# Loads that fill both halves of the partitions from the same 64 rows, issued as two transfers instead of one

## The chip, the cores and the metric

The kernel runs on one core of a Trainium2 chip. The metric is the time of one execution in microseconds (us) on the device, as the median of several runs; lower is better. The engines are TensorE (PE, with its weight loads PEld), VectorE (DVE), ScalarE (ACT), GpSimd (POOL) and SyncE (SP). SP does no arithmetic here: it issues every transfer (DMA) of the program, one after the other, and its issues appear in the profile as SPq. 16 DMA engines move the data.

## What is computed

Three parts follow one another: a recurrence with a state of 40 x 40 for each of 32 (batch, head) pairs over 768 steps, and two gated layers over 3072 tokens of 320 values.

```python
# r, k, v, w, a, b: (4, 8, 768, 40), float32
for t in range(S):
    y[:, :, t] = np.einsum('bhd,bhde->bhe', rt, state)
    Sa = np.einsum('bhde,bhe->bhd', state, at)
    state_decay = state * wt[:, :, None, :] - np.einsum('bhd,bhe->bhde', Sa, bt)
    state = state_decay + np.einsum('bhd,bhe->bhde', vt, kt)
# y as (3072, 320) goes into layer 1, its result into layer 2
h = x @ w_in                      # (320, 2048)
g = h * np.clip(h + 3, 0, 6) / 6  # layer 1;  layer 2: g = h / (1 + exp(-h))
out = g @ w_out                   # (2048, 320)
```

The four weight matrices arrive as 64-bit numbers.

## The kernel before

The recurrence is worked in chunks of 32 steps, which turns it into matmuls and one triangular inverse for each chunk and head. Four chunks are a window of 128 steps of two batches (16 heads); there are 12 windows (`NN`) and 48 chunks. For each window:

- `prepare` (lines 299 to 375) loads the inputs of the window (`in_pre`), forms running products of the decay, and writes them to scratch in DRAM (`scr_w`, `scr_a`, `scr_kb`).
- `windows` (434) forms the 64 triangular factors (16 heads x 4 chunks) of 32 x 32 on PE and writes them to `scr_l` as 64 rows of 1024 numbers.
- `factors` (479) loads `scr_l` into `u`, the same 64 rows into partitions 0 to 63 and again into 64 to 127. There are two buffers for `u`; the second lies in the tile `stage`, and its loads read `stage<-scr_l` in the trace. ScalarE (in window 0 also VectorE) copies the even columns for the lower and the odd ones for the upper half into `uh` (line 509 and 506), and VectorE solves the triangles in 60 short instructions (515 and 519). So both halves of the partitions work on one problem, each on every other column.
- `solved` (529) writes the inverses to `scr_t` and loads them into `ga` (line 540). `ga` has three buffers, one for each of three windows in a row.
- `steps` (569) is the recurrence itself. Each chunk begins with matmuls on `rhs` and `ga` (line 602) and ends with the new state in `rhs`; the next chunk needs it. Its small loads are `rhs<-in_vt` (546), `vr<-in_vr` (550) and `ysr<-in_rt` (565).

Beside the recurrence run the conversion of layer 1's weights (`raws` and `convert`, lines 719 to 797: 16 blocks, each with `raw0` from `w_in` and `raw1` from `w_out`, turned from 64-bit numbers into a sum of two float32 ones), `inputs1` (855), which loads a window's result from `scr_y` and its decay from `scr_w` as layer 1's input, and layer 1 itself (`first`, line 927, and `second`, line 971) for the windows that are done. A row of `w_in` or of the input has 320 values, which are two and a half times 128; the last 64 rows are put on both halves of the partitions, so that one matmul over 128 rows can take two products of them. After the last chunk, `phase2` converts layer 2's weights in the same way (`stage<-in_w2i`, `stage<-in_w2o`), while PE finishes layer 1; then layer 2 runs. `raw0` has one buffer in that stage: the load of a block waits until the conversion of the block before has read it.

The order of all instructions is set at build time. Every piece of work is a generator that yields the engine, a cost and the events that it waits for; `Order.run` picks what can start first, then by priority, and emits it. For SP the yielded number is a count of bytes. The planner charges each issue 525 ns of SP and adds the bytes divided by a rate. On the chip each engine, SP included, then takes its instructions strictly in this order, and an instruction that has to wait holds up all behind it.

Four places read a source twice with `unsqueeze(0).to_broadcast([2, ...])`, one transfer for both halves of the partitions: line 489 (12 loads), line 735 (32 loads: 16 blocks in each of the two layers), line 869 (24) and line 874 (12). They are the places of the diff.

Of the kernel before, what the change touches and what calls it, by code (L numbers as in the profile page):

```python
# [20 lines left out]
G = NB * H  # L21
HP = H // 2
NW, WT, CT = 6, 128, 32
NC = WT // CT
# [7 lines left out]
DM, DFF = H * D, 2048  # L32
NM = DFF // 128
MT = NB * WT
# [215 lines left out]
class Kernel:  # L250
# [228 lines left out]
    def factors(self):  # L479

        nc, o = self.nc, self.o
        for n in range(NN):
            k = n % 2 if n > 1 else 0
            u = self.u[k]
            free = [("uo", n - 1) if n < 3 else ("iv", n - 2)] if n else []
            if k:
                free += self.converted
            el = yield ("sp", 524e3, ("lo", n), *free)
            nc.sync.dma_start(out=u.rearrange("p j i -> p (j i)"),
                              in_=self.scr_l[n % 2].unsqueeze(0).to_broadcast([2, G * NC, CT * CT]))  # L490
            o.ev[("u", n)] = o.t["sp"]
            o.ev[("ul", n)] = el

# [225 lines left out]
    def raws(self, wi, wo, key):  # L719

        nc, cv = self.nc, self.cv
        for m in range(NM):
            if wi.dtype == mybir.dt.float32:
                k, wiv, wov = 1, wi, wo
            else:
                k, wiv, wov = 2, wi.bitcast(I32), wo.bitcast(I32)
            cs = slice(m * 128 * k, (m + 1) * 128 * k)
            raw, free = self.slot("raw0", key, m)
            raw = raw.bitcast(wiv.dtype)
            yield ("sp", 131e3 * k, free and ("cv", key, free[0], 0), ("u", 0) if key == 1 and m >= GR else None,  # L730
                   ("uo", NN - 1) if key == 2 else None)
            nc.sync.dma_start(out=raw[:, 0:256 * k].rearrange("p (j f) -> p j f", j=2),
                              in_=wiv[0:256, cs].rearrange("(j p) f -> p j f", p=128))
            e = yield ("sp", 66e3 * k)
            nc.sync.dma_start(
                out=raw[:, 256 * k:384 * k],
                in_=wiv[256:320, cs].unsqueeze(0).to_broadcast([2, 64, 128 * k]))
            self.o.ev[("raw", key, m, 0)] = e
            raw, free = self.slot("raw1", key, m)
            raw = raw.bitcast(wiv.dtype)  # L740
            e = yield ("sp", 164e3 * k, free and ("cv", key, free[0], 1))
            nc.sync.dma_start(out=raw[:, 0:DM * k], in_=wov[m * 128:(m + 1) * 128])
            self.o.ev[("raw", key, m, 1)] = e
# [111 lines left out]
    def inputs1(self):  # L855

        nc, o = self.nc, self.o
        xs = self.xw[0].rearrange("p (j b t) -> p j b t", j=3, b=NB)
        ws = self.xw[1].rearrange("p (j b t) -> p j b t", j=3, b=NB)
        xf, wf = (x.rearrange("p (j n) -> p j n", j=3) for x in self.xw)  # L860
        for n in range(NN):
            free = ("xp", n - 1) if n else ("cv", 1, K0 - 1, 1)
            sw, sy = self.scr_w[n], self.scr_y[n]
            for b in range(NB):
                r = sw[b * DM:(b + 1) * DM, 0:WT]
                yield ("sp", 131e3, ("wo", n), free, ("cv", 1, K0 - 1, 0))
                nc.sync.dma_start(out=ws[:, 0:2, b], in_=r[0:256].rearrange("(j p) t -> p j t", p=128))
                yield ("sp", 66e3)
                nc.sync.dma_start(out=ws[:, 2, b], in_=r[256:DM].unsqueeze(0).to_broadcast([2, 64, WT]))
            g = n * NC + NC - 1  # L870
            e1 = yield ("sp", 262e3, *[("yo", g - q, b) for b in range(NB) for q in (0, 2)])
            nc.sync.dma_start(out=xf[:, 0:2], in_=sy[0:256].rearrange("(j p) b t -> p j (b t)", p=128))
            e = yield ("sp", 131e3)
            nc.sync.dma_start(out=xf[:, 2],
                              in_=sy[256:DM].rearrange("p b t -> p (b t)").unsqueeze(0).to_broadcast([2, 64, MT]))
            xh, xl = self.xh[n % 2], self.xl[n % 2]
            e = yield ("pool", 1750.0, e, e1)
            nc.gpsimd.tensor_tensor(out=xf, in0=xf, in1=wf, op=ALU.mult)
            e = yield ("act", 740.0, e, ("g1", n - 2) if n > 1 else None)
            nc.scalar.activation(out=xh, in_=xf, func=AF.Copy)  # L880
            yield ("pool", 1230.0, e)
            nc.gpsimd.tensor_tensor(out=xl, in0=xf[:, 0:2], in1=xh[:, 0:2].bitcast(F32), op=ALU.subtract)
            e = yield ("pool", 640.0)
            nc.gpsimd.tensor_tensor(out=xh[64:128, 2], in0=xf[64:128, 2], in1=xh[64:128, 2].bitcast(F32),
                                    op=ALU.subtract)
            o.ev[("xp", n)] = o.ev[("x", n)] = e
# [317 lines left out]
```

## Time and profile before

| | us |
|---|---|
| median of 3 runs | 1398.6 |
| lowest and highest of them | 1393.26, 1407.38 |
| the profiled execution | 1414.4 |
| its span, first to last instruction | 1412.6 |
| PE busy in it | 1126.7 (80%) |
| DVE, ACT, POOL busy | 823.1, 636.1, 399.4 |
| mean granted clock of PE | 0.902 |

The profile is of one execution, and all its times are in us from the start of the span. A row of the timeline has the start, the duration, the engine, the line of the kernel, the operation, the tile written and the tiles read; in brackets stands how long the engine was idle before it and what ended the idleness. A row of SPq shows how long the issue took on SP, not how long the transfer took. A row of the windows has for each stretch the busy time of PE, PEld, DVE, ACT and POOL, in this order, with the number of their instructions, the granted clock of PE (1.00 is full speed), the share of the 16 DMA engines' time that was busy, and what they moved.

### The profile page before, as it was taken

The page shows a single profiled execution, that of the slowest core. Times are in us where ns is not written, and L with a number is a line of the kernel's source. Part 1 is how long each engine was busy: PE and PEld are TensorE (multiplying, and loading weights), DVE is VectorE, ACT ScalarE, POOL GpSimd, SP SyncE. Part 2 cuts the span into 40 slices and gives each one's busy share as a digit, 9 for nine tenths or more (in the row PEclk, how much of TensorE's full clock was granted, in tenths as well). Part 3 has the DMA queues.
Part 4 walks back from the last instruction along what each step waited for, and adds up shares of the span by engine and source line. Part 5 has one row for each costly group of instructions (what it writes and reads, how often), then busy time and mean ns, then how long its engine had stood idle before and what let it go on. Part 6 is the DMA issues. An engine that isn't in the chain of part 4 may idle for free. (4 is left out here: it accounts for less than half of the span.)

```text
span 1412.6 us, 31488 instructions
## 1 busy us (share of the span) xinstructions
PE 1126.7 (80%) x12278; PEld 1048.3 (74%) x12278; DVE 823.1 (58%) x1948; ACT 636.1 (45%) x1369; POOL 399.4 (28%) x485
## 2 busy tenths in 40 slices
PE   2035348877878877989768989997789999999998
PEld 1034247777778766877767878887779999999997
DVE  6495857557578784965877968458882222322221
ACT  3224435643533534655244456655663333433333
POOL 6333443515324231333331413346550000000000
PEclk9999667879988967997888899999999999999999
DMA  6566765534676564375765743345441000100000
GB/s 198 153 149 151 176 144 118 111 103 112 153 175 142 126 163 124 82 151 151 175 140 129 169 106 97 87 102 111 108 94 44 21 21 22 40 24 21 22 10 22
DMA packets 276414, 150.03 MB, mean 106 GB/s; under 512 B 176032, under 2 KB 257568, under 8 KB 276256
## 3 DMA queue, kind: packets, MB, share of 16 engines
q1 hardware_dynamic: 276256, 147.92, 43.7%
q8 instruction: 99, 1.62, 0.5%
q14 instruction: 59, 0.48, 0.1%
HBM read 113.24 MB, written 34.63 MB: 105 GB/s over the span
## 5 line engine op out<-in xcount | busy, mean ns | idle before, releaser
L971 PE MATMUL po<-w,gh 128*128 128x320 f32 x1536 | 400.5, 328 | 22.7 <-ACT xo L987 19.7
L927 PE MATMUL ph<-xh,w 128*128 128x256 f32 x2304 | 387.5, 298 | 26.9 <-DVE t L942 26.0
L927 PEld LDWEIGHTS ph<-xh,w 128*128 128x128 f32 x2304 | 330.2, 201 | 37.8 <-DVE t L942 28.8
L971 PEld LDWEIGHTS po<-w,gh 128*128 128x128 f32 x1536 | 281.3, 199 | 32.0 <-ACT xo L987 21.5
L971 PE MATMUL po<-w,gl 128*128 128x320 f32 x768 | 248.2, 323 | 11.1 <-DVE gl L953 7.1
L953 DVE TENSOR_TENSOR gl<-t,gh 128x512 fp32r<-128x512 f32 x118 | 88.9, 756 | 246.7 <-ACT gh L947 246.4
L947 ACT ACTIVATE gh<-t 128x512 fp32r<-128x512 f32 x192 | 120.8, 630 | 99.4 <-DVE t L942 90.0
L927 PE MATMUL ph<-xl,w 128*128 128x256 f32 x768 | 164.5, 297 | 0.0
L971 PEld LDWEIGHTS po<-w,gl 128*128 128x128 f32 x768 | 153.3, 200 | 14.9 <-DVE gl L953 10.3
L950 POOL TENSOR_TENSOR gl<-t,gh 128x512 fp32r<-128x512 f32 x74 | 95.2, 1288 | 183.5 <-ACT gh L947 149.8
L944 ACT ACTIVATE t<-ph 128x512 f32<-128x512 f32 x96 | 57.2, 596 | 186.8 <-PE ph L927 186.8
L519 DVE TENSOR_TENSOR uh<-uh,ut 128x30 f32<-128x30 f32 (+4 forms) x360 | 129.2, 359 | 10.5
L643 DVE STREAM_TRANSPOSE vr<-r 64x128 f32<-64x128 f32 x192 | 61.2, 319 | 125.0 <-ACT ysl L619 47.7
L927 PEld LDWEIGHTS ph<-xl,w 128*128 128x128 f32 x768 | 127.3, 201 | 2.5 <-issue 0.3
L602 PE MATMUL r<-rhs,ga 104*32 104x40 f32 x1536 | 75.1, 215 | 63.0 <-DMA ga<-scr_t 30.5
L602 PEld LDWEIGHTS r<-rhs,ga 104*32 104x32 f32 x1536 | 68.1, 123 | 72.1 <-issue 45.4
L563 POOL COPY ysr<-rhs 32x320 f32<-32x320 f32 x96 | 43.6, 460 | 212.4 <-PE r L681 151.4
L515 DVE TENSOR_TENSOR ut<-uh,u 128x30 f32<-128x30 f32 (+7 forms) x210 | 72.6, 346 | 29.5 <-ACT uh L509 23.7
L637 ACT ACTIVATE ysr<-r 32x160 f32<-32x160 f32 x192 | 57.2, 298 | 65.7 <-DVE vr L643 54.4
L654 PE MATMUL r<-vr 104*64 104x64 f32 x768 | 50.3, 272 | 36.6 <-DVE vr L643 25.8
L940 ACT ACTIVATE t<-ph,con 128x512 f32<-128x512 f32 x96 | 65.3, 683 | 28.8 <-PE ph L927 27.1
L681 PE MATMUL r<-ysr,ysl 104*40 104x72 f32 x1536 | 67.2, 248 | 11.9 <-DVE ysr L664 6.1
(119 smaller groups left out, 1500.4 us busy)
## 6 DMA issues: line engine op xcount, KB each, us to landing
vr<-in_vr SPq DMA_DIRECT2D x96, 208.0 KB
ld<-in_pre SPq DMA_DIRECT2D x12, 960.0 KB
s<-scr_kb SPq DMA_DIRECT2D x46, 160.0 KB
ld<-scr_kb SPq DMA_DIRECT2D x40, 160.0 KB
stage<-in_w2o SPq DMA_DIRECT2D x16, 320.0 KB
scr_kb<-ld SPq DMA_DIRECT2D x12, 384.0 KB
scr_x<-xo SPq DMA_DIRECT2D x24, 192.0 KB
xw<-scr_x SPq DMA_DIRECT2D x48, 96.0 KB
```

The source lines that it names most:

```text
L515: nc.vector.tensor_tensor(out=tv, in0=uh[:, 0:r, j:j + 1].to_broadcast([128, r, m]), in1=u[:, j:j + 1, j + 1:CT].to_broadcast([128, r, m]) ...
L519: nc.vector.tensor_tensor(out=uh[:, 0:r, j + 1:CT], in0=uh[:, 0:r, j + 1:CT], in1=tv, op=ALU.add)
L602: nc.tensor.matmul(out=pv[32:64, h], lhsT=ga[0:KP, b * H + h, c * CT:(c + 1) * CT], rhs=self.rhs[b][0:KP, h], start=True, stop=True)
L637: nc.scalar.activation(out=self.ysr[b][32:64, q::2, CT:RW], in_=pv[E0 + 32 * q:E0 + 32 * q + 32, :, 0:D], func=AF.Copy)
L643: nc.vector.transpose(out=self.vr[b][64 * q:64 * q + 64, :, 1], in_=pv[E0:E0 + 64, :, 32 * q:32 * q + 32])
L681: nc.tensor.matmul(out=pv[E0 * u:E0 * u + D, h], lhsT=self.ysl[b][0:KP, 4 * u + h], rhs=self.ysr[b][0:KP, 4 * u + h], start=True, stop=True)
L927: nc.tensor.matmul(out=p[:, h * MT:(h + 1) * MT], lhsT=seq[q][0], rhs=seq[q][1], start=q == 0, stop=q == 7)
L940: nc.scalar.activation(out=t, in_=p, func=AF.Relu, bias=self.three)
L947: nc.scalar.activation(out=gh, in_=t, func=AF.Copy)
L950: nc.gpsimd.tensor_tensor(out=gl, in0=t, in1=gh.bitcast(F32), op=ALU.subtract)
L953: nc.vector.tensor_tensor(out=gl, in0=t, in1=gh.bitcast(F32), op=ALU.subtract)
L971: nc.tensor.matmul(out=self.po[s], lhsT=l, rhs=r, start=m == 0 and q == 0, stop=m == NM - 1 and q == 2)
```

## The change

Each of the four loads becomes a loop over the two halves of the partitions, with one transfer of 64 rows for each. The bytes yielded to the planner are halved for each of the two (written as 66e3 for 131e3 in the last). What is loaded, where it goes and who waits for it stay the same.

```diff
@@ factors
-            el = yield ("sp", 524e3, ("lo", n), *free)
-            nc.sync.dma_start(out=u.rearrange("p j i -> p (j i)"),
-                              in_=self.scr_l[n % 2].unsqueeze(0).to_broadcast([2, G * NC, CT * CT]))
+            for x in range(2):
+                el = yield ("sp", 262e3, ("lo", n), *free)
+                nc.sync.dma_start(out=u[64 * x:64 * x + 64].rearrange("p j i -> p (j i)"), in_=self.scr_l[n % 2])
@@ raws
-            e = yield ("sp", 66e3 * k)
-            nc.sync.dma_start(
-                out=raw[:, 256 * k:384 * k],
-                in_=wiv[256:320, cs].unsqueeze(0).to_broadcast([2, 64, 128 * k]))
+            for x in range(2):
+                e = yield ("sp", 33e3 * k)
+                nc.sync.dma_start(out=raw[64 * x:64 * x + 64, 256 * k:384 * k], in_=wiv[256:320, cs])
@@ inputs1
-                yield ("sp", 66e3)
-                nc.sync.dma_start(out=ws[:, 2, b], in_=r[256:DM].unsqueeze(0).to_broadcast([2, 64, WT]))
+                for x in range(2):
+                    yield ("sp", 33e3)
+                    nc.sync.dma_start(out=ws[64 * x:64 * x + 64, 2, b], in_=r[256:DM])
...
-            e = yield ("sp", 131e3)
-            nc.sync.dma_start(out=xf[:, 2],
-                              in_=sy[256:DM].rearrange("p b t -> p (b t)").unsqueeze(0).to_broadcast([2, 64, MT]))
+            for x in range(2):
+                e = yield ("sp", 66e3)
+                nc.sync.dma_start(out=xf[64 * x:64 * x + 64, 2], in_=sy[256:DM].rearrange("p b t -> p (b t)"))
```

Because there are more steps for SP, the planner lays the order of all engines anew. The first place is SP's queue around the load of `u` for window 2; `scr_t<-uh` and `ga_139<-scr_t` are the inverse of window 1 on its way to PE. Before:

```order
L535 DMA scr_t<-uh 1024x1x32 x2
L872 DMA xw_103<-scr_y 128x2x256
L732 DMA stage<-in_w1i 128x2x256
L489 DMA u<-scr_l 128x1x1024
L540 DMA ga_139<-scr_t 32x64x32
L735 DMA stage<-in_w1i 128x1x256
L742 DMA stage<-in_w1o 128x640
```

And with the change (the lines of the kernel from `factors` on have shifted by one or two):

```order
L535 DMA scr_t<-uh 1024x1x32
L711 DMA scr_y<-rx_137 40x8x64
L535 DMA scr_t<-uh 1024x1x32
L872 DMA xw_103<-scr_y 128x2x256
L490 DMA u<-scr_l 64x1024 x2
L540 DMA ga_139<-scr_t 32x64x32
L342 DMA scr_w<-ld 128x5x129
L346 DMA scr_a<-ld 128x5x128
L732 DMA stage<-in_w1i 128x2x256
L736 DMA stage<-in_w1i 64x256
```

The load of `u` is two rows of the queue (x2), and `ga_139` still stands right behind it; the weights' load `stage<-in_w1i` has moved behind both.

The second place is SP's queue where layer 2's weights begin to be loaded, after the last chunk of the recurrence. Before:

```order
L732 DMA stage<-in_w2i 128x2x256
L735 DMA stage<-in_w2i 128x1x256
L742 DMA stage<-in_w2o 128x640
L1011 DMA scr_x_66<-xo 128x384
L872 DMA xw_103<-scr_y 128x2x256
L874 DMA xw_103<-scr_y 128x1x256
L732 DMA stage<-in_w2i 128x2x256
L735 DMA stage<-in_w2i 128x1x256
```

And with the change:

```order
L732 DMA stage<-in_w2i 128x2x256
L736 DMA stage<-in_w2i 64x256 x2
L741 DMA stage<-in_w2o 128x640
L872 DMA xw_103<-scr_y 128x2x256
L875 DMA xw_103<-scr_y 64x256 x2
L732 DMA stage<-in_w2i 128x2x256
L736 DMA stage<-in_w2i 64x256 x2
```

Each broadcast has become two issues in its place, and the store of a result (`scr_x`) is no longer between the first two blocks.

## Rows read from the trace of the kernel before

**Rows 1.** Windows by stage: stretch, length, busy us per engine, clock, DMA share, GB/s

```profile
0.00:200.00 200.00, 60.23 (x804) 51.21 (x804) 130.44 (x337) 68.89 (x156) 84.48 (x115) 0.88 0.63 161
200.00:931.00 731.00, 617.54 (x8166) 554.82 (x8167) 504.76 (x1340) 357.70 (x831) 241.39 (x304) 0.86 0.56 131
931.00:1062.00 131.00, 104.82 (x705) 99.02 (x703) 102.72 (x148) 77.44 (x160) 73.55 (x68) 0.95 0.48 105
1062.00:1412.60 350.60, 344.13 (x2607) 343.28 (x2606) 85.18 (x124) 132.09 (x224) 0.00 (x0) 1.00 0.09 24
```

**Rows 2.** Chain of waits, 931 to 1062 us: shares by line

```profile
by line: DMA stage<-in_w2i 55.0%; ACT stage L770 6.6%; issue 5.7%; DMA stage<-in_w2o 5.2%; DVE stage L779 4.2%; DMA xw<-scr_y 4.0%; DVE gl L953 2.7%; DVE stage L791 2.3%; DMA scr_x<-xo 1.6%; DVE tix L776 1.6%; DVE stage L776 1.5%; SPq L732 
```

**Rows 3.** Timeline around the load of u for window 0

```profile
43.83 0.52 SPq L489 DMA_DIRECT2D u<-scr_l  x1
...
48.44 10.39 SPq L742 DMA_DIRECT2D xw<-in_w1o  x1
58.44 0.63 ACT L509 ACTIVATE uh<-u 64x512 f32<-64x512 f32 x1 [12.99 <-DMA u<-scr_l]
```

**Rows 4.** DMA issues: transfer, engine, operation, count, KB of each

```profile
u<-scr_l SPq DMA_DIRECT2D x7, 512.0 KB
...
ga<-in_pre SPq DMA_DIRECT2D x4, 322.5 KB
```

**Rows 5.** Windows inside the load of u for window 0

```profile
46.00:48.00 2.00, 0.00 (x0) 0.00 (x0) 0.00 (x0) 0.00 (x0) 0.38 (x1) 1.00 1.00 317
...
52.00:54.00 2.00, 0.00 (x0) 0.00 (x0) 0.00 (x0) 0.00 (x0) 0.00 (x0) 1.00 0.13 51
```

**Rows 6.** Timeline at the start: a load of 128 rows, its user

```profile
1.21 0.42 SPq L317 DMA_DIRECT2D ga<-in_pre  x1
...
4.70 1.72 DVE L325 TENSOR_SCALAR ld<-ga 128x640 f32<-128x640 f32 x1 [4.70 <-DMA ga<-in_pre]
```

**Rows 7.** Timeline around the load of u for window 1

```profile
103.38 0.52 SPq L489 DMA_DIRECT2D u<-scr_l  x1
...
116.79 0.63 ACT L509 ACTIVATE uh<-u 64x512 f32<-64x512 f32 x1 [9.19 <-DMA u<-scr_l]
...
117.79 1.27 PE L602 MATMUL r<-rhs,ga 104*32 104x40 f32 x16 [9.65 <-ACT rhs L698]
```

**Rows 8.** Timeline around the load of u for window 2

```profile
171.63 0.58 SPq L489 DMA_DIRECT2D u<-scr_l  x1
...
172.31 0.42 SPq L540 DMA_DIRECT2D ga<-scr_t  x1
...
186.40 2.31 PE L602 MATMUL r<-rhs,ga 104*32 104x40 f32 x32 [23.79 <-DMA ga<-scr_t]
```

**Rows 9.** Windows of 16 us from nine loads of u: first, last, sum

```profile
277.70:293.70 16.00, 8.30 (x99) 7.44 (x101) 1.55 (x5) 5.06 (x13) 5.55 (x8) 0.61 0.37 105
...
820.10:836.10 16.00, 11.46 (x176) 10.01 (x172) 6.41 (x19) 5.88 (x14) 0.89 (x2) 0.89 0.35 89
sum 144.00, PE 89.28 PEld 79.50 DVE 65.51 ACT 47.13 POOL 42.73; mean PE 9.92 PEld 8.83 DVE 7.28 ACT 5.24 POOL 4.75
```

**Rows 10.** Timeline around the load of u for window 7

```profile
543.57 0.59 SPq L489 DMA_DIRECT2D stage<-scr_l  x1
...
551.43 7.47 SPq L546 DMA_DIRECT2D rhs<-in_vt  x2
...
557.28 1.24 PE L602 MATMUL r<-rhs,ga 104*32 104x40 f32 x16 [10.33 <-DMA rhs<-in_vt]
```

**Rows 11.** Windows: a stretch without a load of u

```profile
600.00:650.00 50.00, 45.99 (x713) 40.70 (x712) 28.81 (x74) 25.77 (x65) 16.41 (x24) 0.93 0.71 156
```

**Rows 12.** Timeline of one block of layer 2's weights

```profile
936.94 0.54 SPq L735 DMA_DIRECT2D stage<-in_w2i  x1
...
943.98 0.56 ACT L770 ACTIVATE stage<-stage 128x384 f32<-128x384 f32 x1 [2.01 <-DMA stage<-in_w2i]
```

**Rows 13.** Line 735: its issues, duration ns min/median/max

```profile
L735 SPq DMA_DIRECT2D stage<-in_w2i x16: 526/527/609, 929.0 to 1046.5; - x16
```

## Prediction, made before the change was run

> **What bounds the kernel now.** I read first the windows by stage, to see how busy TensorE (PE) is. [rows 1] cut the span where its character changes. From 1062 us to the end PE is busy 344.13 of 350.60 us at clock 1.00: nothing is to be had there. Before that PE stands idle for 139.8 us of the first 200, for 113.5 of the next 731, and for 26.2 of the 131 in which the second layer's weights are converted. The program must finish the same matmuls in any case, so what the change can be worth is idle PE time in these three stages, plus time that PE spent at the lower of its two clock levels (1.2 instead of 2.4 GHz) after such idleness: the granted clock of the long stage is 0.86, a mean over stretches at 0.50 and at 1.00.
>
> Next I asked who is waited for, beginning with the chain of waits of 931 to 1062 us. [rows 2] give 55.0% of this stretch, 72 us, to the transfer `stage<-in_w2i`. Then I went to the loads that the diff names, in order of time, and read there the transfer queue's instructions (SPq) and the first user of the data. The load of `u` for window 0 is issued at 43.83 us and ScalarE starts on it at 58.44, after an idle time of 12.99 us [rows 3]: 14.6 us for 512 KB [rows 4]. Further, an issue behind it, `xw<-in_w1o`, holds the queue for 10.39 us instead of about half a microsecond, so that everything behind that is late too.
>
> Why so slow? [rows 5] are the windows inside that load. At 46 to 48 us, while loads issued after it run beside it, the share of the 16 DMA engines is 1.00 with 317 GB/s. At 52 to 54 us only `u` is left, and the share is 0.13 with 51 GB/s. 0.13 of 16 is two engines. 524,288 bytes at 51 GB/s are 10.3 us; at 317 GB/s they would be 1.7 us. So a load with the pattern "64 rows to both halves" runs on two engines, and whatever is queued on those two behind it waits.
>
> **The change part by part.** Each of the 80 broadcast loads (12 of `u`, 32 of `raw0`, 24 and 12 of `inputs1`) becomes two loads of 64 rows. The trace has no 64-row load, so its price is bounded from both sides. Upper end: it is as slow as now, 13 to 15 us for `u`. Lower end: the nearest wide load, `ga<-in_pre` with 128 rows and 322.5 KB [rows 4], is issued at 1.21 us and its user starts at 4.70 [rows 6], 3.5 us. I take the lower end plus one more issue of 0.53 to 0.6 us, with some traffic beside it: 4.6 us from the first issue, because the row next to it in size and queue is this one and since 0.13 of the engines is the peculiarity of the broadcast.
>
> The Trainium skill (DMA: Bandwidth & Descriptors, Rules for kernel authors) says that an outermost step-0 broadcast of c copies confines a transfer to c engines, and that an outer dimension divisible by 16 uses all 16. By this rule a half of 64 rows runs on 16 engines; the share of 0.13 agrees for the broadcast, and no run here shows the half yet. The same table speaks against the change: two transfers to disjoint partition halves are not worth it, since both spread over the same 16 engines and serialize, and one 128-partition transfer is to be used. By that alone the sum would be only the added issues; the trace differs in its premise, for the one transfer replaced here holds 0.13 of the engines.
>
> First 200 us. (a) Window 0: from 43.8 to 58.4 us PE has no work, and VectorE and ScalarE are waiting for `u` [rows 3, 5]. 14.6 - 4.6 = 10 us, all on the path, since VectorE's inversion follows directly. (b) Window 1: issued 103.38, used 116.79, and PE's next step waits 9.65 us behind ScalarE, which sat on this load [rows 7]: 13.4 - 4.6 = 9 us. (c) Window 2: `ga<-scr_t` for window 1 is issued right behind the `u` load, at 172.31, and PE waits 23.79 us for it until 186.40 [rows 8], 14.1 us after the issue; in the changed order it still stands right behind `u`. Two engines finish the broadcast only shortly before; without it I allow 6 us. 14.1 - 6 = 8 us. Sum: -27 us.
>
> 200 to 931 us, nine further `u` loads. [rows 9] are stretches of 16 us from each issue: PE is busy 89.28 of 144 us, 54.7 idle. Outside them the stage has 113.5 - 54.7 = 58.8 us of idle time in 587, a tenth. At that rate 144 us would have 14, so 40 are excess. The load of window 7 shows how: `u` is issued at 543.57, an issue of `rhs<-in_vt` behind it lasts 7.47 us, and PE waits 10.33 us for `rhs` [rows 10]. Behind `rhs` comes the next step of the recurrence. I take three quarters of the excess, -30 us, since other small transfers end some of these waits soon after. The clock: the mean of the nine stretches is 0.80 (their nine values added and divided), so the other 587 us have (0.86 x 731 - 0.80 x 144) / 587 = 0.875, and the stretch 600 to 650, with no `u` load in it, has 0.93 and PE busy 45.99 of 50 [rows 11]. With 0.875 throughout, 617.5 us of PE work shrink by 1.7%, 10.6 us; I take -8.
>
> 931 to 1062 us. One period is: broadcast issued at 936.94, first user at 943.98 [rows 12], 7.0 us; with 0.53 for the added issue [rows 13] and 3.0 for landing it is 3.5. Over 15 periods 52 us leave the transfer chain. But PE has 104.82 us and VectorE 102.72 us of work in this stretch [rows 1], so it cannot fall below 105, and 26 us is the most. VectorE then becomes what is late: nine tenths busy, with waits between it, ScalarE and GpSimd. I take half, -14 us.
>
> Costs. 80 issues of 0.53 to 0.6 us are 42 to 48 us of the queue's time. Those of the first terms are already in the 4.6 us; most others lie under PE work. I add +4 us for steps that stand behind one on the queue. The two `inputs1` loads are costed at nothing: they prefetch behind the recurrence; if that cover goes, they gain rather than lose.
>
> Sum: -27 - 30 - 8 - 14 + 4 = -75 us. Span 1412.6 - 75 = 1337.6, and with the 1.8 us around it 1339.4 in terms of the profiled execution's 1414.4. The median of the runs shown is 1398.6, 1.1% lower, so I scale: 1339.4 x 1398.6 / 1414.4 = 1324 us.
>
> **The rivals.** Another wait takes the place. The nine stretches stay idle, as the recurrence also waits for other transfers of short rows and the planner laid its order anew. What speaks for it: PE idles a tenth of the time outside the stretches too. Against: with no such load PE is 92% busy [rows 11]. Then the first 200 us and half of the last term remain: -27 - 7 + 4 = -30, or 1368 us. Chance 0.15.
>
> Deeper. All excess goes, the clock reaches 0.89, the conversion falls to 107 us and the start gains 32: -32 - 55 - 20 - 24 = -131, or 1269 us. For it: the queue's long issues also come behind `raw0`. Against: VectorE's 102.72 us and the added issues. Chance 0.14 for under 1285.
>
> The order eats it. The planner's sequence differs from the first windows on; a step placed later than now could cost in the long stage what the start gains. Within 1%, about 1395 us. Chance 0.06.
>
> Slower: the queue becomes the bound. If the halves go one behind the other and land no earlier than the one transfer did (the price above at its upper end, also the case in which the change doesn't do what it says), nothing is gained, and the in-order queue carries 80 more issues, up to 48 us of it on the path: 1398.6 + 45 = 1443 us. It decides from the point where `u` lands more than 13.4 us after its first issue. For it: already now issues queue behind one another [rows 10]. Against: a share of 0.13 leaves fourteen engines free. Chance 0.04. The Trainium skill's rule on disjoint halves (DMA: Bandwidth & Descriptors, Rules for kernel authors), taken alone, would be this case.
>
> **How the numbers follow.** The forecast, 1285 to 1350 us, has 0.61. The low end of the range, 1272, is close to the deeper case; the high end, 1372, holds the first rival with 1368. Left out are half of the deeper case (0.07), a little of the first rival (0.02), and the last two (0.10). Faster by over 1% (about what a measurement of this kernel can tell from no change): 0.61 + 0.15 + 0.14 = 0.90; within 1%: 0.06; slower: 0.04.
>
> **What would show it.** Right: no window beside a `u` load with a DMA share of 0.13; ScalarE's first copy 4 to 6 us after the issue; PE's 23.79 us wait for `ga<-scr_t` under 17; no issue of 5 to 12 us behind `u`; the recurrence's end near 870 us instead of 931; `stage<-in_w2i` no longer the largest in the chain after it, but VectorE. Wrong: `u` still lands after 10 us or more, or it lands early and PE's idle time in the middle stage stays over 100 us.

## The result and the profile after

The changed kernel takes 1283.0 us (median of 4 runs, 1281.2 to 1287.6), the kernel before 1400.1 in the same comparison; the ratio is 0.9168, 95% interval 0.9114 to 0.9221. So it is 8.3% faster; 1324 was forecast, with 1272 to 1372 as the range.

To see where the time left, both traces are cut at the same events rather than at the same times: the first matmul of the fifth chunk (line 602), which is the first one that needs window 1's inverse; the matmul of the flag that is formed after the last chunk (line 1031); and ScalarE's first instruction for layer 2 (line 944). The windows of the kernel before, cut so (columns as in [rows 1]):

```profile
0.00:186.40 186.40, 53.14 (x708) 45.09 (x709) 121.43 (x315) 63.65 (x144) 79.93 (x111) 0.90 0.62 160
186.40:928.40 742.00, 622.03 (x8242) 558.41 (x8242) 512.93 (x1360) 361.22 (x840) 245.51 (x306) 0.85 0.56 131
928.40:1048.90 120.50, 97.61 (x661) 92.05 (x660) 93.93 (x137) 70.56 (x146) 67.58 (x62) 0.96 0.51 113
1048.90:1412.60 363.70, 353.94 (x2668) 352.79 (x2668) 94.81 (x138) 140.69 (x241) 6.40 (x7) 0.99 0.09 25
```

And those of the changed kernel:

```profile
0.00:149.20 149.20, 53.28 (x708) 45.69 (x709) 125.85 (x315) 63.52 (x143) 76.10 (x105) 0.91 0.77 199
149.20:810.70 661.50, 596.31 (x8264) 533.82 (x8264) 516.51 (x1361) 362.59 (x844) 249.03 (x314) 0.91 0.63 148
810.70:916.20 105.50, 91.74 (x639) 87.22 (x639) 97.08 (x130) 65.09 (x136) 64.14 (x57) 0.97 0.40 120
916.20:1280.40 364.20, 353.25 (x2672) 351.57 (x2670) 99.47 (x144) 143.09 (x246) 10.57 (x11) 1.00 0.09 27
```

Of 132.2 us of span, 37.2 left the start, 80.5 the long stage, 15.0 the stage of layer 2's weights, and nothing the last one. That is more than the 117 us between the medians, as the profiled execution of the kernel before (1414.4 us) was 14 us longer than its median; a stage's difference can be too large by a few us for that reason alone. In the long stage PE's idle time fell from 120.0 to 65.2 us (length less busy time), and its busy time from 622.0 to 596.3 for practically the same matmuls, as the granted clock, a mean over 1.2 and 2.4 GHz, rose from 0.85 to 0.91.

The load of `u` for window 0 in the timeline after; its two issues stand in one row:

```profile
37.41 1.10 SPq L490 DMA_DIRECT2D u<-scr_l  x2
...
40.68 0.63 ACT L509 ACTIVATE uh<-u 64x512 f32<-64x512 f32 x1 [0.97 <-DMA u<-scr_l]
...
41.76 0.42 DVE L506 COPY uh<-u 64x512 f32<-64x512 f32 x1 [2.55 <-DMA u<-scr_l]
```

ScalarE has the lower half 3.3 us after the first issue and VectorE the upper one 4.35 us after it, in place of 14.6 [rows 3]. Over all 12 loads the landing, the last landing signal counted from the first issue, takes 5.3 us in the mean (4.3 to 7.4), before 13.9 (12.5 to 15.6). The windows beside it, the counterpart of [rows 5]:

```profile
38.00:40.00 2.00, 0.00 (x0) 0.00 (x0) 1.21 (x1) 0.47 (x1) 1.68 (x4) 1.00 0.63 182
40.00:42.00 2.00, 0.00 (x0) 0.00 (x0) 0.24 (x1) 0.63 (x1) 0.65 (x1) 1.00 1.05 280
42.00:44.00 2.00, 0.00 (x0) 0.00 (x0) 1.05 (x5) 0.08 (x1) 0.00 (x0) 1.00 1.01 365
```

The stretch with a share of 0.13 is gone; from 40 to 44 us the share is 1.05 and 1.01. At window 2, `ga` behind `u`, the counterpart of [rows 8]:

```profile
142.48 1.13 SPq L490 DMA_DIRECT2D u<-scr_l  x2
143.71 0.53 SPq L540 DMA_DIRECT2D ga<-scr_t  x1
...
149.22 2.31 PE L602 MATMUL r<-rhs,ga 104*32 104x40 f32 x32 [13.88 <-DMA ga<-scr_t]
```

From issue to PE 5.5 us, not 14.1; the idle time before it is 13.88 us, not 23.79.

The traces also record the signals with which each transfer reports that its data have landed; the views printed here do not list them. Each of the 80 broadcasts has one 0.4 to 0.6 us after its issue ends and two when its data land; each of the 160 halves has 16. Read as one signal for each DMA engine that moves a part, these are the two engines of the share of 0.13, and all 16 for a half. The signals also show who waits behind whom: of the 16 of `ga<-scr_t` at window 2, issued behind the broadcast of `u` at 172.31 us, 14 come by 176.9 us and the last two at 186.1 and 186.3, just after `u` at 185.0. With the change all 16 come within 0.7 us (148.4 to 149.1).

And the 16 us from each of the nine later loads of `u` (223.4 to 710.7 us; first, eighth, and the sum over nine), which answer to [rows 9]:

```profile
223.44:239.44 16.00, 15.43 (x234) 13.13 (x234) 8.55 (x26) 11.92 (x29) 6.82 (x9) 1.00 0.61 178
...
671.70:687.70 16.00, 16.00 (x200) 14.01 (x201) 8.78 (x24) 10.02 (x23) 10.15 (x16) 0.71 0.70 178
...
sum 144.00, PE 134.91 PEld 120.65 DVE 107.81 ACT 88.34 POOL 61.69; mean PE 14.99 PEld 13.41 DVE 11.98 ACT 9.82 POOL 6.85
```

PE is busy 134.9 of 144 us, before 89.3. The chain of waits in the stage of layer 2's weights, shares by line:

```profile
by line: issue 16.7%; DVE gl L953 11.9%; DVE t L942 8.8%; DVE stage L778 8.8%; DVE stage L775 8.8%; DVE stage L790 8.3%; DMA stage<-in_w2i 7.7%; PE po L971 5.0%; DVE tix L775 4.4%; DVE tix L790 3.6%; DVE tix L778 3.4%; ACT gh L947 2.7%; PE 
```

`stage<-in_w2i` had 55.0% [rows 2] and has 7.7%; VectorE's lines lead, and VectorE is busy 97.08 of the 105.5 us.

### The profile page after: what moved, and what is told of

Read it like the earlier page. It is cut to its first block, busy times and chain, and to the rows that moved or that the text cites. A ratio compares the mean times of both kernels' runs of the same rounds, so it can differ in the third digit from the quotient of the medians.

```text
span 1280.4 us, 31616 instructions
## 1 busy us (share of the span) xinstructions
PE 1094.6 (85%) x12278; PEld 1018.3 (80%) x12278; DVE 838.9 (66%) x1948; ACT 634.3 (50%) x1369; POOL 399.8 (31%) x485
## 4 chain that ended last, share of the span: by engine, by line
PE 48%; DVE 13%; DMA 4%; issue 3%; ACT 2%; SPq 1%; POOL 1%; DVEq 0%; ACTq 0%; POOLq 0%
PE ph L927 19%; PE po L971 18%; PE r L602 3%; PE r L630 2%; DVE ut L515 2%; DVE t L942 2%; DVE uh L519 2%; PE r L681 2%; PE r L616 2%; PE r L654 1%; DMA vr<-in_vr 1%; DVE gl L953 1%; DMA stage<-in_w2i 1%; DVE stage L778 1%; DVE stage L775 1%
## 5 line engine op out<-in xcount | busy, mean ns | idle before, releaser
L927 PE MATMUL ph<-xh,w 128*128 128x256 f32 x2304 | 381.6, 293 | 18.5 <-DVE t L942 17.4
L971 PE MATMUL po<-w,gh 128*128 128x320 f32 x1536 | 390.8, 321 | 3.5 <-ACT xo L987 3.2
L927 PEld LDWEIGHTS ph<-xh,w 128*128 128x128 f32 x2304 | 323.6, 197 | 29.3 <-DVE t L942 20.4
L971 PEld LDWEIGHTS po<-w,gh 128*128 128x128 f32 x1536 | 274.2, 194 | 11.6 <-ACT xo L987 4.3
L971 PE MATMUL po<-w,gl 128*128 128x320 f32 x768 | 244.7, 319 | 13.8 <-DVE gl L953 9.7
L971 PEld LDWEIGHTS po<-w,gl 128*128 128x128 f32 x768 | 149.2, 194 | 18.9 <-DVE gl L953 13.1
L927 PE MATMUL ph<-xl,w 128*128 128x256 f32 x768 | 161.6, 293 | 0.0
L927 PEld LDWEIGHTS ph<-xl,w 128*128 128x128 f32 x768 | 124.6, 197 | 2.6 <-issue 0.2
L940 ACT ACTIVATE t<-ph,con 128x512 f32<-128x512 f32 x96 | 65.5, 683 | 17.9 <-PE ph L927 13.9
L559 ACT ACTIVATE ysl<-kbn,con 64x320 f32<-64x320 f32 x96 | 52.8, 557 | 42.7 <-PE r L681 41.2
```

What stands on the lines that cost most here:

```text
L927: nc.tensor.matmul(out=p[:, h * MT:(h + 1) * MT], lhsT=seq[q][0], rhs=seq[q][1], start=q == 0, stop=q == 7)
L940: nc.scalar.activation(out=t, in_=p, func=AF.Relu, bias=self.three)
L971: nc.tensor.matmul(out=self.po[s], lhsT=l, rhs=r, start=m == 0 and q == 0, stop=m == NM - 1 and q == 2)
```

## Experiments

Two theories at first. T: the gain comes from transfers that run on all 16 DMA engines instead of two. O: the planner's new order brings a good part of it. "Order of before" below means that a load's transfers are issued in one step of the planner, with the old byte count, so that all else keeps its place.

**All four loads split, order of before.** The edit, at each place as here:

```diff
             el = yield ("sp", 524e3, ("lo", n), *free)
-            nc.sync.dma_start(out=u.rearrange("p j i -> p (j i)"),
-                              in_=self.scr_l[n % 2].unsqueeze(0).to_broadcast([2, G * NC, CT * CT]))
+            for x in range(2):
+                nc.sync.dma_start(out=u[64 * x:64 * x + 64].rearrange("p j i -> p (j i)"), in_=self.scr_l[n % 2])
```

> All four loads are split, but both halves are issued in one planner step, so that every engine keeps the order of the kernel before. Theory T (the gain comes from transfers that use all DMA engines): 1275 to 1300 us, as with the change. Rival O (the planner's new order brings 30 us or more of it): 1310 to 1340 us.

Measured: 1298.2 us, ratio 0.9263 (0.9214 to 0.9312). Inside T's bounds, and one per cent above the changed kernel.

**The new order with the old transfers.** The edit to the changed kernel, again at all four places:

```diff
             for x in range(2):
                 el = yield ("sp", 262e3, ("lo", n), *free)
-                nc.sync.dma_start(out=u[64 * x:64 * x + 64].rearrange("p j i -> p (j i)"), in_=self.scr_l[n % 2])
+                if x == 0:
+                    continue
+                nc.sync.dma_start(out=u.rearrange("p j i -> p (j i)"),
+                                  in_=self.scr_l[n % 2].unsqueeze(0).to_broadcast([2, G * NC, CT * CT]))
```

> The changed kernel's order, but each pair of halves is again the one broadcast transfer, issued where the second half stood. Theory T: 1385 to 1420 us, nothing gained against before, and u lands 13 to 15 us after its issue. Rival O: 1350 to 1370 us.

Measured: 1390.4 us, ratio 0.9898 (0.9863 to 0.9932). `u` for window 0 is issued at 42.23 us and used at 57.01, 14.8 us later. So the order brings 1.0%, with the old transfers as with the new ones (0.9168 over 0.9263 is 0.990, though those two intervals overlap a little). T holds for the bulk; of the 117 us the order has some 14.

**Only `u` split, order of before.** The first diff at `factors` alone.

> Only the 12 loads of u are split, in the order of before. Theory T as the prediction sized it (u brings 65 of its 75 us net of the weights' stage): about three quarters of the gain of 117 us, so 1305 to 1330 us, and the stage of layer 2's weights stays at 131 us. Rival R (the many small loads of raw0 and inputs1, which also lie on two engines, bring as much as u): 1340 to 1365 us.

Measured: 1323.3 us, ratio 0.9422 (0.9377 to 0.9466), inside T's bounds, with seven tenths of the gain (5.8 of 8.3%). Its windows up to the end of the recurrence, and the sum over the 16 us from each of its nine later loads of `u`:

```profile
0.00:159.40 159.40, 53.33 (x708) 45.24 (x709) 122.30 (x315) 63.52 (x144) 75.20 (x102) 0.91 0.75 187
159.40:840.90 681.50, 600.07 (x8243) 537.05 (x8244) 522.12 (x1360) 360.52 (x840) 250.88 (x316) 0.90 0.62 143
...
sum 144.00, PE 129.02 PEld 115.92 DVE 103.57 ACT 82.41 POOL 52.85; mean PE 14.34 PEld 12.88 DVE 11.51 ACT 9.16 POOL 5.87
```

The start is 27.0 us shorter, the long stage 60.5; of this 38.6 are idle time of PE (120.0 to 81.4) and 22.0 busy time, with the clock at 0.90 for 0.85. The stage of layer 2's weights has 118.6 us, practically as before (120.5 in this cut). `u` lands 5.9 us after its first issue in the mean of the 12 (4.5 to 8.2).

**`u` in halves without a broadcast, but on two engines.** Is it the splitting, the missing broadcast, or the number of engines? The edit, against the one just before:

```diff
             for x in range(2):
+                for r0, r1 in ((0, 62), (62, 64)):
+                    nc.sync.dma_start(out=u[64 * x + r0:64 * x + r1].rearrange("p j i -> p (j i)"),
+                                      in_=self.scr_l[n % 2, r0:r1])
-                nc.sync.dma_start(out=u[64 * x:64 * x + 64].rearrange("p j i -> p (j i)"), in_=self.scr_l[n % 2])
```

> As the one before, but each half of u is loaded as 62 and 2 rows, so four transfers without any broadcast. Theory T, with the Trainium skill's rule on how many engines a transfer gets (the largest count up to 16 that divides the rows; DMA: Bandwidth & Descriptors, Why a DMA increments its semaphore by 16 and not by 1): 62 and 2 rows run on two engines, the windows inside the load show a DMA share of 0.13 again, u lands 11 to 16 us after its issue, and the time is 1395 to 1425 us. Rival S (splitting or the missing broadcast is what helps): 1300 to 1340 us.

Measured: 1406.1 us, ratio 1.0005 (0.9975 to 1.0034): the whole gain of `u` is gone. The load of window 0 in the timeline, and the windows inside it:

```profile
43.29 1.27 SPq L491 DMA_DIRECT2D u<-scr_l  x4
...
53.74 0.63 ACT L511 ACTIVATE uh<-u 64x512 f32<-64x512 f32 x1 [8.92 <-DMA u<-scr_l]
58.77 0.42 DVE L508 COPY uh<-u 64x512 f32<-64x512 f32 x1 [14.45 <-DMA u<-scr_l]
```

```profile
54.00:56.00 2.00, 0.00 (x0) 0.00 (x0) 0.00 (x0) 0.37 (x1) 0.00 (x0) 1.00 0.12 49
56.00:58.00 2.00, 0.00 (x0) 0.00 (x0) 0.00 (x0) 0.00 (x0) 0.00 (x0) 1.00 0.13 54
```

VectorE gets its half 15.5 us after the first issue (14.3 in the mean of the 12 loads), and the share is 0.12 to 0.13 again, without any broadcast. Each of these transfers has two landing signals, as the broadcast had, besides the one soon after its issue. So neither the splitting nor the missing broadcast is what helps, but how many engines a transfer gets; that four issues in place of two are not the harm is shown by the quarters below. The Trainium skill's rule (DMA: Bandwidth & Descriptors, Why a DMA increments its semaphore by 16 and not by 1), the largest number up to 16 that divides the rows, foretold two engines for 62 rows, and the trace agrees with its 0.12 to 0.13. This kernel also gives a second baseline for the long stage, cut at the same events, since `u` lands in it as late as before:

```profile
186.10:924.20 738.10, 613.88 (x8244) 549.70 (x8244) 514.75 (x1358) 360.52 (x840) 244.86 (x306) 0.87 0.56 132
```

PE is idle for 124.2 us here. Against this trace `u` in halves takes 42.8 us off PE's idle time and 13.8 off its busy time, so of the 22.0 above some 8 are the difference between two executions.

**`u` on one engine.** The last edit with 61 and 3 rows in place of 62 and 2.

> Only u, each half as 61 and 3 rows, in the order of before. By theory T, 61 rows run on one engine: u then takes about 20 us (128 rows of 4 KB at about 0.16 us each, from 10.3 us on two engines for all of them) and lands some 22 us after its issue, 8 us later than before. From 12 loads, whose 9 to 10 us brought 83 us: 70 us more than before, 1450 to 1490 us. Rival (the wait has saturated, what hangs on u is covered further by other work): under 1430 us.

Measured: 1506.5 us, ratio 1.0732 (1.0673 to 1.0790). The mechanism held, its price was set too low: the load lands 23.2 us after its first issue in the mean of the 12, 9.3 later than before, and the program takes 102 us more. The 61 rows have one landing signal besides the early one. Window 0:

```profile
43.36 1.36 SPq L491 DMA_DIRECT2D u<-scr_l  x4
44.77 7.41 SPq L317 DMA_DIRECT2D ga<-in_pre  x1
...
66.54 0.42 DVE L508 COPY uh<-u 64x512 f32<-64x512 f32 x1 [22.13 <-DMA u<-scr_l]
```

It is used 23.2 us after the issue, and even the issue right behind it is held, for 7.41 us. Little covers a slow `u`: 9.3 us more per load cost 102 / 12 = 8.5 us each, as the 8.1 us (13.92 to 5.85) that a load had gained brought 83 / 12 = 6.9. These prices hold what is queued behind `u` too, not its own readers alone.

**Only `raw0` split, order of before.** The first diff, at `raws` alone.

> Only the 32 loads of raw0 are split, in the order of before. The runs so far leave about 25 us for raw0 and inputs1 together. Theory A (the gains add up, and raw0 has most of that rest, in the first 200 us and in the stage of layer 2's weights): 1370 to 1385 us; the stage of layer 2's weights, from the last step of the recurrence to layer 2's first activation, falls from 120 to about 110 us. Rival B (raw0 alone is hidden behind the slow u): within 1% of before, 1392 to 1410 us.

Measured: 1373.4 us, ratio 0.9764 (0.9711 to 0.9817): theory A. Its windows:

```profile
0.00:171.80 171.80, 54.50 (x709) 46.44 (x710) 122.53 (x315) 63.77 (x144) 80.25 (x111) 1.00 0.68 173
171.80:904.50 732.70, 620.43 (x8242) 557.32 (x8242) 513.92 (x1360) 361.35 (x840) 244.18 (x306) 0.87 0.56 133
904.50:1014.80 110.30, 95.53 (x657) 91.33 (x657) 100.31 (x137) 69.37 (x147) 68.49 (x62) 0.95 0.42 123
```

14.6 us shorter at the start, 9.3 in the long stage, 10.2 in the stage of layer 2's weights. The first of these the prediction did not have at all. The second is no more than what kernels with the old `raw0` show in that stage (738.1 with 62 rows, 731.8 with `inputs1` split, next), so it is not shown to be a gain.

**Only `inputs1` split, order of before.** The first diff, at the two loads of `inputs1` alone.

> Only the 36 loads of inputs1 are split, in the order of before. The prediction costed them at nothing: 1395 to 1412 us. Rival (they occupy the same two engines 36 times in the long stage and hold up what is queued behind): 1370 to 1390 us.

Measured: 1398.5 us, ratio 0.9960 (0.9932 to 0.9988). As good as nothing, as costed; half a per cent may be there. The three parts multiply to 0.9422 x 0.9764 x 0.9960 = 0.916, all together give 0.926: they add up except for about one per cent.

**Quarters instead of halves, order of before.** All four loads as four transfers of 32 rows, here against the halves:

```diff
+            for x in range(4):
+                nc.sync.dma_start(out=u[32 * x:32 * x + 32].rearrange("p j i -> p (j i)"),
+                                  in_=self.scr_l[n % 2, 32 * (x % 2):32 * (x % 2) + 32])
-            for x in range(2):
-                nc.sync.dma_start(out=u[64 * x:64 * x + 64].rearrange("p j i -> p (j i)"), in_=self.scr_l[n % 2])
```

> All four loads in the order of before, each as four transfers of 32 rows instead of two of 64: 160 more issues than with halves, 85 to 95 us more of the queue's time. Theory T: halves already use all engines, and most issues lie under other work, so 1298 us and up to 15 more: 1298 to 1315 us. Rival Q (the in-order queue is close to being the bound, each issue costs its own time): 1340 to 1390 us.

Measured: 1296.5 us, ratio 0.9224 (0.9176 to 0.9272), just under T's range and the same as with halves (0.9263). 160 more issues cost nothing that can be measured; the queue isn't the bound.

**Can more be had the same way?** Three kernels on top of the changed one, in its order. `vr` has 104 rows, and `ad`, `s`, `ysr` and `ga<-scr_a` have 40; each is cut so that its larger part has a multiple of 16 rows, for example:

```diff
-                    nc.sync.dma_start(out=ad[E0 * x:E0 * x + D, :, x], in_=sa[x])
+                    for r0, r1 in ((0, 32), (32, D)):
+                        nc.sync.dma_start(out=ad[E0 * x + r0:E0 * x + r1, :, x], in_=sa[x][r0:r1])
```

> The changed kernel with the 96 loads of vr (104 rows) issued as 96 and 8 rows, in one planner step. If the rule of the largest divisor holds, 104 rows run on 13 engines and 96 on 16. Theory: the rings of these 13 still hold up other transfers: 1268 to 1280 us. Rival: with u gone no group of engines is the bound, and 96 more issues bring nothing: 1280 to 1290 us.

> The changed kernel with the loads of 40 rows into ad, s, ysr and ga issued as 32 and 8 rows, in one planner step (by the same rule 10 engines become 16 and 8). Theory: 1268 to 1280 us. Rival: 1280 to 1295 us, some 190 more issues cost a little and bring nothing.

> Both of the two before it. Theory: 1255 to 1275 us. Rival: 1280 to 1300 us.

Measured: 1281.7 us, ratio 0.9125 (0.9077 to 0.9173), for `vr`; 1301.7, 0.9239 (0.9202 to 0.9276), for the rows of 40; 1305.6, 0.9285 (0.9250 to 0.9320), for both. By their landing signals the loads of 104 rows have 13 engines and those of 40 rows 10; cut, the larger parts have 16 and the 8 rows 8. The kernel before took 1406.3 us in this comparison and 1400.1 in that of the changed kernel, so the ratios are to be compared. For the rows of 40 the rival holds: 0.8% slower than the changed kernel (0.9168, 0.9114 to 0.9221), with intervals that overlap a little, and 1.3% with both cuts, clear of it. `vr` is undecided: 0.5% better, inside the noise, and its interval reaches into what the theory gave and into what the rival gave. No version beats the changed kernel beyond the noise, so it is not shown that transfers on 10 or 13 engines still hold up others.

## Why the prediction was right, and where its sizes were off

The sign, the mechanism and the place were right. The time came out near the low end of the range: 1283 lies just under 1285, so it is what the second rival ("deeper", 0.14) described, and not the forecast's own 1285 to 1350. Against that rival's terms, the long stage lost 54.8 us of idle time (55 was named) and 25.7 of busy time (20), the start 37.2 (32) and layer 2's conversion 15.0 (24): the sum agrees in part because the last term was too large and two others too small. By the forecast's own terms:

- *Landing of `u`, 4.6 us.* 4.35 us at window 0, 5.3 in the mean of the 12. Right, and the runs show the cause: 62 rows on two engines undo it.
- *Start, -27.* With `u` alone it is 27.0 us, and not by chance: its three parts, 10, 9 and 8, were 10.1 and 7.9 in the landing of `u` and 8.6 in the way from `ga`'s issue to PE. But -37.2 were measured: the `raw0` loads had no term here. Their broadcasts stood behind the first loads of `u` on the same two engines (the one issued at 45.86 us, beside window 0's `u`, lands at 65.2, while `xw<-in_w1o`, issued after it, has 14 of its 16 signals by 61.3), and splitting them alone takes 14.6 us off the start. The prediction saw their long issues and named them only for the rival.
- *Long stage, -30 for idle time.* In the nine stretches `u` alone takes PE's idle time from 54.7 to 15.0 us, 39.7 of the 40 that were called excess, and outside them it stays (65.3 before, 66.5 after, in the event cut); the step "I take three quarters of the excess, -30 us, since other small transfers end some of these waits soon after" was too cautious. There was no next wait close behind: PE is 90% busy in those stretches with `u` alone and 94% with the whole change, which takes 54.8 us of idle time off the stage.
- *Clock, -8.* This is the term that was most wrong by its factor. `u` alone takes 14 to 22 us off PE's busy time (by the two baselines), the whole change 25.7. The step "0.875 throughout" took the mean outside the 16 us stretches as what could be reached; the mean after is 0.90 with `u` alone and 0.91 with all. Outside the nine stretches the clock rose from 0.86 to 0.90 with `u` alone although the idle time there stayed, which points to time at the lower level outside them that followed from the gaps inside; no run separates it.
- *Layer 2's weights, -14.* -15.0. Splitting `raw0` alone brings 10.2; the other 5 come with the new order (keeping the old one leaves 110.5 us). VectorE is what is late, as forecast.
- *Costs, +4.* None was found. Quarters add 160 issues for nothing. Adding up the durations of all of SP's transfer issues in the traces gives 638 us before and 544 after, although there are 80 more: 28 issues lasted over 3 us before (138 us together), 4 after (16 us). Issues held behind a transfer on few engines were what cost SP this time: the sum is 543 with `u` alone in halves, 623 with its 62 rows and 759 with 61.
- *The order.* It was feared as a loss ("the order eats it", 0.06) and brings 1.0%.

The signs that were named came where they are read here, two of them further than said: ScalarE's first copy starts 3.3 us after the issue (4 to 6 was said), and the recurrence ends at 810.7 us (870). No issue in the whole trace lasts 5 us. One sum is off by a microsecond: the first rival, scaled as the forecast is, gives 1369.

The rival that ends slower, and with it the Trainium skill's rule on two transfers to disjoint halves (DMA: Bandwidth & Descriptors, Rules for kernel authors), is refuted for this case: two halves in place of the 128-row broadcast give 0.9422 at `u` alone. The halves of `u` do come one after the other, 1.1 us apart; the rule doesn't reach a transfer that has only two engines. That each of the two halves runs on all 16 is read from its 16 landing signals.

What stays open is why the cut of the 40-row loads costs 0.8%, if it is more than noise: its 204 additional issues are no explanation by themselves, as 160 cost nothing in the quarters. In its one trace the long stage has 685.5 us, 24 more than in the changed kernel.

## What to carry to other kernels

Look at the DMA share in short windows inside a load that someone waits for: 0.13 of 16 is two engines, and a leading repeat in the source is one way to get there, an unlucky number of rows (62, 61) another. Such a load costs twice, for its own reader and for every transfer queued behind it on the same engines, and PE's work in the long stage took more time too, 622.0 us at a mean clock of 0.85 where it took 596.3 at 0.91. Splitting it is worth many times its issues; cutting transfers that already have 10 or 13 engines brought nothing here that stands out from the noise.

## What the runs showed of the hardware that was not expected

The program's time follows the landing of one load of 512 KB almost us for us, 0.8 to 1.0 us for each us in each of the 12 windows: in their mean it lands after 5.9, 14.3 and 23.2 us with 64, 62 and 61 rows in the first of the transfers of each half, and the program takes 1323, 1406 and 1506 us. Two rows less cost 6%, three 14%. And adding transfers made the issuing engine's total work smaller, 638 to 544 us, because the time for which an issue is held counts as well: one of line 735 for `stage<-in_w1i` lasted 12.04 us in the kernel before, while the median of those twelve is 0.59.
